# A third pair rearranged: its state products split over two visits, its values taken with the carried part, a quarter of w_out loaded plainly

## The chip, the cores and the metric

The kernel runs on one core of a Trainium2 chip. The metric is the time of one execution in microseconds (us) as the device measures it. TensorE (PE in the profile, PEld for its weight loads), VectorE (DVE), ScalarE (ACT), GpSimd (POOL) and SyncE (SP) each run their own list of instructions in order; SP and POOL also issue the DMAs.

## The reference

A block-wise linear attention with decay feeds a two-layer network. What is computed, shortened:

```python
# q, k, v: 4 batches, 8 heads, 768 tokens, 64 wide; blocks of 64 tokens
intra = (qb @ kb^T * Dmask) @ vb                 # Dmask[i, j] = lam ** (i - j) for i >= j, else 0
inter = (qb * lam ** (pos + 1)) @ kv_state
out_block = intra + inter
kv_state = lam ** 64 * kv_state + (kb * lam ** (63 - pos))^T @ vb
x = out, heads side by side                      # 3072 x 512
h = x @ w_in                                     # w_in: 512 x 2048
result = (h * cos(h)) @ w_out                    # w_out: 2048 x 512, result 3072 x 512
```

All inputs and the result are float32; the kernel multiplies in bfloat16.

## The kernel before, in words

**Tiling.** The 3072 tokens are 24 blocks of 128, taken two at a time: pair `pr` holds blocks `2*pr` and `2*pr+1`, the same chunk of two batches. Pairs 0 and 1 are made in another way ("spans", `add_span`). Pair 2 is the third pair, the first that goes the general way. The network works on tiles of `TILES = [4, 2, 2, 2, 2, 4, 4, 4]` blocks: tile 0 is the two spans, tile 1 is pair 2, tile 2 is pair 3, tile 3 is pair 4.

**One pair.** q, k and v of a block are loaded in float32 on SP's queue (L253, 256 KB each). q and v are scaled and all three become bfloat16 (`prepare`, L329 to L337; v as `v_s`). q and k are transposed into `qkT`, for pair 2 by TensorE (L359, 8 matmuls for q and 8 for k, copied out by DVE at L362), later by DMA (L365). On TensorE there follow: the scores (L407, 32 small matmuls), masked by DVE into `s_m` (L412); the state products, `update` (L419, 16 small matmuls for each 64-token half, "half 0" and "half 1"), added up by DVE (L425) into `sum` or into `S` in bfloat16; the values, half of them across the row halves of the output and half along them (`values` and the head of `values_carried`, L470, 16 small matmuls each); and the carried part, the state times q (L502). The output goes to `xT` (L510).

**One tile of the network.** `add_ffn`: `ps_h` = w_in times xT (L732, 16 groups of 4 matmuls), cos on ACT (L738), `g` on DVE (L744), then for each block `ps_f` = g times w_out (L779, 16 matmuls of 128x512, in groups of 4), copied to `o_sb` (L793) and stored. A group of 4 `ps_f` needs one quarter of w_out and four parts of g.

**Visits.** The pair's small matmuls use a quarter of the array, the network's all of it. A run of small matmuls between network matmuls is called a visit here. In the steady state one visit holds the values of a pair, the scores and state products of the next, and then the rest of the values and the carried part. Between the two halves of the values a 1x1 copy on DVE (`turn`, L487) must have read the first. Where a pair has no next one in its visit and no `turn`, `values_carried` puts a drain of TensorE there instead; no pair of the kernel before comes to that line.

**The third pair is special.** Its `add_stretch` is called with `ahead=first_update`: its first values share a visit with its own state products, and the second values share one with the carried part. Its scores follow the state product of the spans, L697. The state of the spans is copied by ACT (L701) and made bfloat16 by POOL (L704).

**Order of work.** A planner (`Planner.order`) sets each engine's order when the program is built: each step has a cost, what it depends on, a priority, PSUM banks and buffers, and the step that can start first is put next. `then` ties a step to the one that must follow it on its engine. The chip obeys only the order and the semaphores. `T_LAT` holds the planner's figures for the landing of the DMA transposes and thereby shifts where scores are placed.

**Loads.** `ORDER` names the early loads: q4, q5, k4, k5, v4, v5 are pair 2's blocks; i0 to i5 are w_in's parts and o0 to o3 w_out's quarters, issued by POOL, which turns float32 into bfloat16 during the DMA. o3 waits on POOL until q4 has landed, and SP issues v4 only when k4 has landed. q4 waits for a step of the network (`pace`).

Of the kernel before, what the change touches and what calls it, by code (L numbers as in the profile page):

```python
# [10 lines left out]
F32 = mybir.dt.float32  # L11
# [15 lines left out]
ALONE = [3, 4]  # L27
T_LAT = {3: 2.46, 4: 4.62, 5: 3.15, 6: 4.42, 7: 3.9, 8: 3.84, 9: 6.24, 10: 5.52, 11: 4.89}
HELD = (10,) * 12
# [7 lines left out]
STATE_OUT = [("ACT", "ACT"), ("ACT", "ACT")]  # L37
ORDER = "q0 k0 q1 k1 v0 v1 i0 i1 i2 i3 i4 i5 o0 o1 o2 q4 q5 k4 k5 o3"

# [107 lines left out]
def kernel(  # L147
# [127 lines left out]
    def add_load(n, name, src, prio, deps=()):  # L275
        b, c = where(n)

        def emit(_):
            t = loads.tile([P, H, D], F32, tag=name, name=name)
            live[name, n] = t  # L280
            i = start(nc.sync, t, src[b, :, c * P:(c + 1) * P, :].transpose([1, 0, 2]), deps)
            if (name, n) == ("q_f", 2 * SPANS):

                tc.add_manual_dep(i.ins, pace[0].ins.ins.name, mybir.DependencyInfo(
                    mybir.DependencyClass.Sync, mybir.DependencyReason.DATA), reason="order of loads")
            return i

        issue_t[name, n], load_t[name, n] = dma("SP", LOAD_US, 0.85, emit, prio, deps, get=name,
                                                lat=1.9 if name == "v_f" and n < 2 * SPANS + 2 else 1.0)
        return load_t[name, n]  # L290
# [3 lines left out]
    def add_w(which, c, prio, deps=()):  # L294
        def emit(_):
            if which == "in":
                a, z = sum(W_IN[:c]) * P, sum(W_IN[:c + 1]) * P
                return start(nc.gpsimd, w_in_sb[:, :, a:z], w_in_src[:, :, a:z], deps)
            a, z = c * KF // WCH, (c + 1) * KF // WCH
            return start(nc.gpsimd, w_out_sb[:, a:z, :], w_out_src[:, a:z, :], deps)  # L300

        part = W_IN[c] / 4 if which == "in" else 1.0
        early = which == "in" and c < 3
        _, w_t[which, c] = dma("POOL", 2.68 * part, 0.8, emit, -2000.0 if early else prio, deps,
                               lat=1.2)
        return w_t[which, c]

    T, So, Vo, d_t, Uo, Uo_sp = ({} for _ in range(6))
# [6 lines left out]
    def prepare(pr):  # L315
# [51 lines left out]
        for i, src in enumerate((a, k_)):  # L367
            get = None if i else "qkT"
            if 2 * pr >= DMA_FROM:
                head, T[pr, i] = dma("SP", 1.4, 1.3, partial(transposes_dma, i=i), 2 * pr + i - LAG + 1.5,  # L370
                                     src + ([qkT_head[pr]] if i else []), get=get, ordered=False)
                T[pr, i].lat = T_LAT.get(pr, 1.2)
                if i and 2 * pr + LAG < NBLK:
                    issue_t["q_f", 2 * pr + LAG].deps.append(head)
            else:
                t = pl.add("PE", MM(P, 8), src + ([T[pr, 0]] if i else []), partial(transposes, i=i), pa(-0.05 + 0.05 * i), banks=1)
                head = T[pr, i] = pl.add("DVE", 0.7, [t], partial(transposes_out, i=i), pa(0.0), get=get)
                t.bank_frees = [[head]]
            if i == 0:
                qkT_head[pr] = head  # L380
        qk_head[pr] = a[0]

    QUART = 0.0317
    first_sum = None

# [8 lines left out]
    def add_scores(pr, part):  # L394
# [3 lines left out]
        last, early = c == NB - 1, pr == SPANS  # L398
        nonlocal first_sum

        def scores(t):
# [11 lines left out]

        def update(t):
            live["kv", pr] = [bank(i, [P, H, D], F32, "ps_kv") for i in t.bank]
            for h in range(H):
                for s, r in enumerate(halves):
                    for m, kv in list(zip(halves, live["kv", pr]))[:1 if last else 2]:
                        nc.tensor.matmul(kv[r, h, :], lhsT=live["qk", pr][m, 1, h, s, :], rhs=live["v_s", 2 * pr + s][m, h, :],  # L419
                                         start=True, stop=True, skip_group_check=True)  # L420
# [15 lines left out]
        s_t.bank_frees = [[So[n0]], [So[n0 + 1]]]  # L436
        u = pl.add("PE", 8 * QUART, [s_t, d_t[n0], d_t[n0 + 1], v12.get(pr - 2)], update, part, banks=1 if last else 2)
        if early:
            u.deps.remove(s_t)
        else:  # L440
            s_t.then = u
        x = pl.add("DVE", 0.69, [u, Uo.get((pr - 1, 1)), Uo.get((pr - 1, 0))], partial(state, half=0, direct=last or early), pa(0.55))
# [3 lines left out]
        if early:  # L446
            x = first_sum = pl.add("DVE", 0.69, [x], partial(state, half=0), pa(0.56))
            u.bank_frees = [[x]]
        if not last:
            y = pl.add("DVE", 0.69, [x], partial(state, half=1), pa(0.57))  # L450
            u.bank_frees.append([y])
            for half, t in enumerate((x, y)):
                if (pr, half) not in Uo:
                    Uo[pr, half] = pl.add("ACT", 0.61, [t], partial(state_16, half=half), pa(0.56 + 0.02 * half))
        qk_head[pr].frees = [T[pr, 0], T[pr, 1], u]
        return s_t, u

    def add_stretch(pr, ahead=None):

# [29 lines left out]
        def values_carried(_):  # L489
            if not more and not apart and not ahead:  # L490
                nc.tensor.drain()
# [39 lines left out]
        apart = pr in APART  # L531
        if ahead:
            v1 = pl.add("PE", 4 * QUART + SW, [So[n0], So[n0 + 1]] + ahead.deps, values, ahead.prio, banks=2)
            v1.then = ahead
            ahead.deps.append(v1)
            chain = []
        else:
            v1 = pl.add("PE", 4 * QUART + SW, deps, values, pa(0.5), banks=2 + 2 * apart)
            chain = [v1]
        if more:  # L540
# [3 lines left out]
            chain += nxt  # L544
        if more or ahead:
            look = pl.add("DVE", 0.12, [v1], turn, pa(-9.0))
            look.worth = 0.45
            deps = deps + [look]
        v2 = v12[pr] = pl.add("PE", (12 if c else 8) * QUART + (SW if ahead else 0.0), deps, values_carried, pa(0.5))
        chain.append(v2)  # L550
# [9 lines left out]
        for s in range(2):  # L560
            So[n0 + s].frees = [v2]
            v_head[n0 + s].frees = [v2]
            if apart:
# [5 lines left out]
        qkT_head[pr].frees = [v2]  # L569
        if (pr + 1, 1) in Uo:  # L570
            Uo[pr + 1, 1].deps.append(v2)
# [144 lines left out]
    def add_ffn(i):  # L716
# [45 lines left out]
        for j in range(nb):  # L762
# [5 lines left out]
            for piece, part in enumerate(pieces):  # L768
                width = part.stop - part.start
                for f0 in range(0, KF, U4):  # L770
                    pr = begins[i + 1] + (j + f0 / KF) * nxt / nb + piece
                    if i == 0 and f0 == KF - U4:
                        pr = begins[i + 1] + (3.75 + 0.05 * j) * nxt / nb

                    def project(task, j=j, f0=f0, piece=piece, part=part, width=width):
                        if f0 == 0:
                            live["f", i, j, piece] = bank(task.bank[0], [P, DM], F32, "ps_f")
                        for f in range(f0, f0 + U4):
                            nc.tensor.matmul(live["f", i, j, piece][:, :width], lhsT=live["g", i][:, f, j * P:(j + 1) * P],  # L779
                                             rhs=w_out_sb[:, f, part], start=(f == 0), stop=(f == KF - 1))  # L780

                    t = pl.add("PE", MM(width, U4), [x for f in range(f0, f0 + U4) for x in gate[f]] + [w_t["out", f0 * WCH // KF], store],
                               project, pr, banks=0 if f0 else 1)
# [20 lines left out]

                eng, queue = ("DVE", "SP") if last and piece == 0 else ("ACT", "ACT" if last else "SP")
                e = pl.add(eng, 0.12 + width / 1060.0, [store], partial(project_out, eng=eng), begins[i + 1] + (j + 1) * nxt / nb,
# [11 lines left out]
    for at, name in enumerate(names):  # L818
# [3 lines left out]
        if name == f"q{2 * SPANS}":  # L822
            deps = []
        if name == f"v{2 * SPANS}":
            deps = [load_t["k_f", 2 * SPANS]]
        if name == "o3":
            deps = [load_t["q_f", 2 * SPANS]]
        if soft:
            kept.append(add_w({"i": "in", "o": "out"}[which], n, at, [] if at < 9 else deps))
# [8 lines left out]
    for pr in range(SPANS, NBLK // 2):  # L838
        prepare(pr)
    first_scores, first_update = add_scores(SPANS, prio_attn(2 * SPANS, 0.2))  # L840
    add_span_state(first_scores, prio_attn(2 * SPANS, 0.2))
    pr = SPANS
    for i in range(len(TILES)):
        while 2 * pr < first[i + 1]:
            if pr + 1 in ALONE:
                add_scores(pr + 1, prio_attn(2 * pr + 2, 0.2))
            add_stretch(pr, first_update if pr == SPANS else None)
            pr += 1
# [4 lines left out]
    closing.deps.append(v12[SPANS])  # L853
    first_sum.deps += Vo[2 * SPANS]
    lead_end = hid[2 * SPLIT]
# [81 lines left out]
```

## Time and profile before

| | |
|---|---|
| median of 3 runs | 202.2 us (201.93 to 202.43) |
| the profiled execution | 202.32 us, of which the span is 200.6 us |
| granted TensorE clock | 1.00 |
| DVE busy | 111.8 us (56%) |
| ACT busy | 116.3 us (58%) |
| POOL busy | 64.7 us (32%) |
| loads and stores of 256 KB on SP's queue | 79, among them 20 each of q, k, v |
| w_out's quarters on POOL's queue | 4, median 12.4 us to landing |

The span runs from the first to the last instruction in the record; 1.72 us lie around it. The ends of matmuls are modelled, their starts are recorded, so distances between starts are the safer reading. An engine's idle time costs something only if it reaches TensorE.

### The profile page before, as it was taken

What the parts mean: (1) busy time and instruction counts of PE and PEld (TensorE: products, weight loads), DVE (VectorE), ACT (ScalarE), POOL (GpSimd) and SP (SyncE); (2) the same over time, 40 slices, a digit from 0 to 9 for tenths busy, and PEclk for the clock granted to TensorE, in tenths of its full rate; (3) what the DMA queues carried; (4) which work ended last, traced back from release to release, by engine and by line L of the source; (5) the groups of instructions that cost most, each with busy time, mean ns of one, the idle gap of its engine ahead of it and who ended that gap; (6) DMA issues with size and microseconds to landing.
All of it is one profiled execution on the core that took longest, in us unless ns stands there. A gap on an engine that the chain in (4) does not pass through costs nothing.

```text
span 200.6 us, 5756 instructions
## 1 busy us (share of the span) xinstructions
PE 195.4 (97%) x2407; PEld 110.2 (55%) x2407; DVE 111.8 (56%) x211; ACT 116.3 (58%) x221; POOL 64.7 (32%) x85
## 2 busy tenths in 40 slices
PE   8799999999999999999999999999999999999994
PEld 2467444547758647867655454544445444444443
DVE  2978772258957816966735679367445454444001
ACT  5878771139768636948654878377455564345120
POOL 5793003066462636372736364003700000000000
DMA  5999999989997999999999899898921010111112
GB/s 161 305 191 204 203 199 215 174 197 227 218 213 172 198 222 199 216 204 187 220 192 242 154 226 178 232 394 197 260 83 51 6 52 3 52 52 52 52 56 105
DMA packets 96620, 33.93 MB, mean 169 GB/s; under 512 B 84690, under 2 KB 93650, under 8 KB 96594
## 3 DMA queue, kind: packets, MB, share of 16 engines
q1 hardware_dynamic: 89088, 28.78, 65.1%
q0 software_dynamic: 7360, 4.72, 16.5%
q8 instruction: 19, 0.31, 0.6%
q10 hardware_dynamic: 146, 0.07, 0.1%
q14 instruction: 7, 0.06, 0.1%
HBM read 27.26 MB, written 6.29 MB: 167 GB/s over the span
## 4 chain that ended last, share of the span: by engine, by line
PE 85%; DMA 9%; SPq 2%; DVE 1%; POOL 1%; ACT 0%; issue 0%; POOLq 0%
PE ps_h L732 41%; PE ps_f L779 36%; DMA v_f<-in_v_dram 4%; DMA sp_f<-in_k_dram 3%; SPq L253 2%; DMA k_f<-in_k_dram 2%; PE ps_o L470 2%; PE ps_o L502 2%; PE ps_kv L419 1%; PE ps_s L407 1%; PE ps_o L638 1%; PE ps_kv L625 1%; POOL k_sp L593 1%; DVE v_s L337 0%; PE ps_t L601 0%
## 5 line engine op out<-in xcount | busy, mean ns | idle before, releaser
L744 DVE TENSOR_TENSOR g<-ps_h,cos 128x256 bf16<-128x256 f32 (+1 forms) x133 | 70.4, 542 | 39.5 <-ACT cos L738 38.3
L779 PE MATMUL ps_f<-w_out_sb,g 128*128 128x512 bf16 (+2 forms) x400 | 90.5, 371 | 0.0
L732 PE MATMUL ps_h<-xT,w_in_sb 128*128 128x256 bf16 (+1 forms) x532 | 89.5, 320 | 0.0
L738 ACT ACTIVATE cos<-ps_h,halfpi 128x256 f32<-128x256 f32 (+1 forms) x133 | 72.1, 571 | 27.6 <-PE ps_h L732 26.3
L732 PEld LDWEIGHTS <-w_in_sb 128*128 128x128 bf16 x532 | 51.5, 98 | 32.9 <-DVE xT L510 0.4
L779 PEld LDWEIGHTS <-g 128*128 128x128 bf16 x400 | 37.5, 98 | 40.4
L329 POOL TENSOR_TENSOR qk<-q_f,q_scale 128x512 bf16<-128x512 f32 x19 | 19.5, 1045 | 38.1 <-DMA q_f<-in_q_dram 31.5
L793 ACT COPY o_sb<-ps_f 128x512 f32<-128x512 f32 (+1 forms) x24 | 13.8, 573 | 24.5 <-PE ps_f L779 24.4
L337 POOL TENSOR_TENSOR v_s<-v_f,v_scale 128x512 bf16<-128x512 f32 x19 | 19.7, 1044 | 10.5 <-DMA v_f<-in_v_dram 10.1
L510 ACT CAST xT<-ps_o 128x512 bf16<-128x512 f32 x15 | 8.1, 588 | 11.5 <-PE ps_o L502 9.1
L412 DVE TENSOR_TENSOR s_m<-ps_s,mask 128x512 bf16<-128x512 f32 x20 | 12.9, 684 | 3.3 <-PE ps_s L407 2.8
L333 POOL CAST qk<-k_f 128x512 bf16<-128x512 f32 x18 | 11.1, 614 | 6.2 <-DMA k_f<-in_k_dram 6.1
L425 DVE TENSOR_TENSOR sum<-sum,ps_kv 128x512 f32<-128x512 f32 x15 | 10.2, 680 | 0.6
L430 ACT CAST S<-sum 128x512 bf16<-128x512 f32 x15 | 9.1, 616 | 2.3 <-DVE sum L425 2.2
L487 DVE COPY spare<-ps_o 1x1 f32<-1x1 f32 x8 | 1.2, 156 | 15.3 <-PE ps_o L470 15.3
L253 POOL DMA_DIRECT2D w_out_sb<-in_moe_w_out_dram x4 | 3.0, 776 | 15.8 <-DMA q_f<-in_q_dram 15.8
L793 DVE COPY o_sb<-ps_f 128x384 f32<-128x384 f32 x1 | 0.6, 556 | 11.5 <-PE ps_f L779 11.5
L470 PEld LDWEIGHTS <-v_s 64*64 64x64 bf16 x320 | 4.2, 106 | 4.6 <-issue 3.2
L470 PE MATMUL ps_o<-s_m,v_s 64*64 64x64 bf16 x288 | 5.9, 197 | 0.1
L617 DVE TENSOR_TENSOR s_m_sp<-ps_s,mask_sp 128x512 bf16<-128x512 f32 x8 | 5.1, 682 | 1.3 <-PE ps_s L612 1.3
L864 PE MATMUL ps_idle<-const-float32-1.0 128*128 128x512 f32 (+1 forms) x6 | 4.8, 893 | 0.8 <-PEq L921 0.8
L502 PE MATMUL ps_o<-qkT,S 64*64 64x64 bf16 x304 | 5.1, 195 | 0.0
(75 smaller groups left out, 83.6 us busy)
## 6 DMA issues: line engine op xcount, KB each, us to landing
q_f<-in_q_dram SPq DMA_DIRECT2D x20, 256.0 KB, 3.8
k_f<-in_k_dram SPq DMA_DIRECT2D x20, 256.0 KB, 4.5
v_f<-in_v_dram SPq DMA_DIRECT2D x20, 256.0 KB, 4.8
out_dram<-o_sb SPq DMA_DIRECT2D x19, 256.0 KB, 2.8
w_out_sb<-in_moe_w_out_dram POOLq DMA_DIRECT2D x4, 512.0 KB, 12.4
sp_f<-in_q_dram SPq DMA_DIRECT2D x2, 512.0 KB, 5.0
sp_f<-in_k_dram SPq DMA_DIRECT2D x2, 512.0 KB, 5.5
w_in_sb<-in_moe_w_in_dram POOLq DMA_DIRECT2D x2, 512.0 KB, 8.8
```

The source lines that it names most:

```text
L329: vec[e].tensor_mul(new_qk()[:, 0, :, s], live.pop(("q_f", 2 * pr + s)), q_scale[:, c, :].unsqueeze(2).to_broadcast([P, H, D]))
L333: (nc.scalar.copy if early else nc.gpsimd.tensor_copy)(new_qk()[:, 1, :, s], live.pop(("k_f", 2 * pr + s)))
L337: vec[e].tensor_mul(live["v_s", 2 * pr + s], live.pop(("v_f", 2 * pr + s)), v_scale[:, c, :].unsqueeze(2).to_broadcast([P, H, D]))
L412: nc.vector.tensor_mul(t, live["s", pr][s], mask.unsqueeze(1).to_broadcast([P, H, D]))
L425: nc.vector.tensor_add(new, live["sum", pr, 0] if half else live["sum", pr - 1, 1], live["kv", pr][half])
L470: yield lambda h=h: nc.tensor.matmul(o[halves[h % 2], h // 2], lhsT=live["v_s", n0 + s][m, h, :], rhs=live["s_m", n0 + s][m, h, :], start= ...
L502: nc.tensor.matmul(live["o", n0 + s][halves[h % 2], h // 2, halves[half]], lhsT=S[r, h, :], rhs=live["qkT", pr][r, 0, h, halves[half]], st ...
L732: nc.tensor.matmul(t[:, :n], lhsT=w_in_sb[:, kd, f * P:(f + 1) * P], rhs=live["xT", i][:, kd, at], start=(kd == 0), stop=(kd == KD - 1))
L738: nc.scalar.activation(c[:, :n], live["h", i, f, at.start][:, :n], AF.Sin, bias=halfpi)
L744: return nc.vector.tensor_mul(live["g", i][:, f, at], live.pop(("h", i, f, at.start))[:, :n], live.pop(("c", i, f, at.start))[:, :n])
L779: nc.tensor.matmul(live["f", i, j, piece][:, :width], lhsT=live["g", i][:, f, j * P:(j + 1) * P], rhs=w_out_sb[:, f, part], start=(f == 0) ...
L793: (nc.scalar.copy if eng == "ACT" else nc.vector.tensor_copy)(o[:, :width], live["f", i, j, piece][:, :width])
```

## The change

- The third pair has no special values step any more. Its scores visit is now: the spans' state product, the scores, and the state product of **half 0** alone. The product of **half 1** moves into the scores visit of pair 3, behind pair 3's scores and ahead of pair 3's own state products.
- Its values and its carried part form one visit. There is no `turn` copy in it; the drain stands between the two halves of the values.
- w_out's last quarter is no longer one converting DMA of POOL. Four plain float32 loads on SP's queue (`w12` to `w15`, 256 KB each, rows of 2 KB) stand behind v5; ACT converts the first, POOL the other three. The last quarter's `ps_f` groups of tile 0 become two groups of two, (12, 13) and (14, 15), for each block.
- v4 is issued without waiting for k4.
- The k transposes of the third pair stand one group of 4 `ps_f` behind its q transposes, where it was two groups.
- One `o_sb` copy (tile 0, block 2) goes from ACT to DVE; the k transposes no longer wait for the copy of the q transposes; some figures of the planner change (`T_LAT`, latencies of loads).

In the built program TensorE's order between the first transposes and tile 1 is, in numbers of matmuls, before: L359 8, ps_f 8, L359 8, ps_f 8, L697 32, L407 32, ps_f 12, L470 16, L419 32, ps_f 4, L470 16, L502 32, ps_f 4. After: L359 8, ps_f 4, L359 8, ps_f 16, L697 32, L407 32, L419 16, ps_f 12, L470 32, L502 32, ps_f 4. Of the 12 `ps_f`, the first 6 use w_out parts 12 and 13, the last 6 parts 14 and 15. Later, pair 3's visit of L407 32, L419 32 becomes L407 32, L419 48, with one more group of 4 `ps_f` ahead of it; pair 4's scores stand 12 `ps_h` and 4 `ps_f` earlier. The numbers of matmuls are the same in all.

```diff
-ORDER = "q0 k0 q1 k1 v0 v1 i0 i1 i2 i3 i4 i5 o0 o1 o2 q4 q5 k4 k5 o3"
+ORDER = "q0 k0 q1 k1 v0 v1 i0 i1 i2 i3 i4 i5 o0 o1 o2 q4 q5 k4 k5 v4 v5 w12 w13 w14 w15"
+WF = ["ACT", "POOL", "POOL", "POOL"]
...
+    def add_w_plain(f, prio):
+        def emit(_):
+            live["w_f", f] = work.tile([P, DM], F32, tag="o_held", bufs=BUFS["o_held"], name="w_f")
+            return nc.sync.dma_start(out=live["w_f", f], in_=w_out_src[:, f, :])
+
+        issue, landed = dma("SP", 0.75, 0.6, emit, prio, get="o_held", lat=1.0)
+        e = WF[f - 12]
+        copy = nc.scalar.copy if e == "ACT" else nc.gpsimd.tensor_copy
+        cast = pl.add(e, 0.61, [landed], lambda _: copy(w_out_sb[:, f, :], live.pop(("w_f", f))), -1.0)
...
-                t = pl.add("PE", MM(P, 8), src + ([T[pr, 0]] if i else []), partial(transposes, i=i), ...)
+                t = pl.add("PE", MM(P, 8), src, partial(transposes, i=i), ...)
...
-        u = pl.add("PE", 8 * QUART, [s_t, d_t[n0], d_t[n0 + 1], v12.get(pr - 2)], update, part, banks=1 if last else 2)
+        sel = [0] if last or early else [0, 1]
+        u = pl.add("PE", 4 * QUART * len(sel), [...], partial(update, sel=sel), part, banks=len(sel))
+        s_t.then = u
         if early:
-            u.deps.remove(s_t)
-        else:
-            s_t.then = u
+            s_t.deps += [d_t[n0], d_t[n0 + 1]]
+        if second_update:
+            rest = second_update.pop()
+            s_t.then, rest.then = rest, u
...
         if not last:
-            y = pl.add("DVE", 0.69, [x], partial(state, half=1), pa(0.57))
+            u1 = pl.add("PE", 4 * QUART, [u], partial(update, sel=[1]), part, banks=1) if early else u
+            y = pl.add("DVE", 0.69, [x, u1], partial(state, half=1), pa(0.57))
+            if early:
+                second_update.append(u1)
...
         def values_carried(_):
-            if not more and not apart and not ahead:
+            if not more and not apart:
                 nc.tensor.drain()
...
-        if ahead:
-            v1 = pl.add("PE", 4 * QUART + SW, [So[n0], So[n0 + 1]] + ahead.deps, values, ahead.prio, banks=2)
-            v1.then = ahead
-            chain = []
-        else:
-            v1 = pl.add("PE", 4 * QUART + SW, deps, values, pa(0.5), banks=2 + 2 * apart)
-            chain = [v1]
+        v1 = pl.add("PE", 4 * QUART + SW, deps, values, pa(0.5), banks=2 + 2 * apart)
+        chain = [v1]
...
-                for f0 in range(0, KF, U4):
+                for f0, nf in [(0, 4), (4, 4), (8, 4), (12, 2), (14, 2)] if i == 0 else [...]:
...
-                eng, queue = ("DVE", "SP") if last and piece == 0 else ("ACT", "ACT" if last else "SP")
+                eng, queue = ("DVE", "SP") if last and piece == 0 or i == 0 and j == 2 else (...)
...
-        if name == f"v{2 * SPANS}":
-            deps = [load_t["k_f", 2 * SPANS]]
-        if name == "o3":
-            deps = [load_t["q_f", 2 * SPANS]]
```

## The prediction

> **What bounds the kernel now.** I read the page's busy times first, then the busy time in stretches, then TensorE's list of instructions where the change lies, then the chain of work that ended last, and last the DMA queues.
>
> ```profile
> PE 195.4 (97%) x2407; PEld 110.2 (55%) x2407; DVE 111.8 (56%) x211; ACT 116.3 (58%) x221; POOL 64.7 (32%) x85
> ```
>
> ```profile
> 30.00:35.00 5.00, 5.00 (x25) 2.26 (x24) 1.26 (x2) 0.62 (x1) 1.81 (x2) 1.00 1.04 216
> 35.00:40.00 5.00, 5.00 (x65) 2.91 (x63) 1.38 (x2) 0.62 (x1) 0.00 (x0) 1.00 1.05 171
> 40.00:45.00 5.00, 4.89 (x130) 2.43 (x126) 2.87 (x5) 1.86 (x4) 2.98 (x4) 1.00 0.87 198
> ```
>
> TensorE is busy in all of a span of 200.6 us but 5.2, and of the stretches from 20 to 180 us only 40 to 45 holds a hole, of 0.11. A busy TensorE is not always one at its best, so I checked the starts: a 128x512 `ps_f` takes 0.216 (24 in 5.18), from 29 us to the end. So little can be gained: the hole, and what a visit of small matmuls costs at its edges. Anything above that must be a new wait.
>
> TensorE around the change (start, us, operation, count):
>
> ```profile
> 34.99 0.61 PE L359 MATMUL ps_t<-ident,qk 128*128 128x128 bf16 x8
> 35.44 1.89 PE L779 MATMUL ps_f<-w_out_sb,g 128*128 128x512 bf16 x8
> 37.17 0.61 PE L359 MATMUL ps_t<-ident,qk 128*128 128x128 bf16 x8
> 37.62 1.89 PE L779 MATMUL ps_f<-w_out_sb,g 128*128 128x512 bf16 x8
> 39.44 0.69 PE L697 MATMUL ps_kv<-v_sp,k_sp 128*64 128x64 bf16 x32
> 40.06 0.44 PE L407 MATMUL ps_s<-qkT 64*64 64x64 bf16 x32
> 40.44 2.76 PE L779 MATMUL ps_f<-w_out_sb,g 128*128 128x512 bf16 x12
> 43.31 0.32 PE L470 MATMUL ps_o<-s_m,v_s 64*64 64x64 bf16 x16
> 43.46 0.43 PE L419 MATMUL ps_kv<-v_s,qk 64*64 64x64 bf16 x32
> 43.82 1.04 PE L779 MATMUL ps_f<-w_out_sb,g 128*128 128x512 bf16 x4
> 44.79 0.32 PE L470 MATMUL ps_o<-s_m,v_s 64*64 64x64 bf16 x16
> 44.94 0.46 PE L502 MATMUL ps_o<-qkT,S 64*64 64x64 bf16 x32
> 45.32 1.04 PE L779 MATMUL ps_f<-w_out_sb,g 128*128 128x512 bf16 x4
> ```
>
> The chain that ended last tells what made the hole: v5, late behind v4, whose issue waited for k4.
>
> ```profile
> 30.08 3.94 DMA k_f<-in_k_dram
> ...
> 34.51 7.98 DMA v_f<-in_v_dram
> 42.49 0.02 issue
> 42.51 0.75 DVE v_s L337
> ```
>
> **Part 1, the visit.** Two visits (43.31 and 44.79) become one. An entry costs 0.11: from 43.82 to 44.79 is 0.97 for four `ps_f` worth 0.86. An exit costs 0.10: L407 to `ps_f` is 0.38 (40.06 to 40.44), L407 to L419, inside a visit, 0.28 (53.31 to 53.59). One of each goes: -0.21. The state products only move: half 0 to the scores visit, half 1 to pair 3's, 16 matmuls of 8 ns each (32 in 0.26), together 0.
>
> **Part 2, the drain.** The joined visit has a drain after its first 16 values, and no row of before has one. The sixteen last 0.32 from first start to last end, and the next start now stands 0.15 behind the first; waiting for the end adds 0.17. The weight loads then start afresh (an L470 load takes 106 ns): +0.28. Bounds: 0, if the waiting hides in the matmuls' own pipeline (a wait can't gain), and 0.49, the whole 0.32 plus 0.11 for weights and 0.06 for a handover (v_s ended at 43.25, L470 began at 43.31). I take 0.28. Behind it on TensorE are 48 small matmuls and the closing `ps_f`; `xT` and tile 1 move with them.
>
> The Trainium skill, "TensorEngine Tiling (Array Packing)", Key Properties, says that a change of tiling mode drains TensorE. By that rule each edge of a visit should itself cost what a drain does, and the joined visit would gain 0.28 where I count 0.21. The edges here cost 0.10 to 0.11, so I stay with the rows.
>
> **Part 3, the hole.** `ps_f` x12 from 40.44, at 0.216 and an entry of 0.11, ends at 43.14; L470 started at 43.31: 0.17 waited for v5's `v_s`. With v5 early this goes: -0.17. What is late next decides the rest.
>
> **Part 4, the loads.** k5 was there at 35.46 (ACT, idle, began its cast at 35.48). v4 now follows at once; the spacing of such loads elsewhere is 1.27 (POOL's starts on q6, q7, k6, k7 and v6 run from 43.45 to 48.54, four steps). v4 is there at 36.7, v5 at 38.0; their casts end at 37.8 (POOL 1.04) and 38.8 (DVE 0.74). The scores visit, which now needs both, comes later (below): covered by 1.4.
>
> Then w12 to w15, 0.262 MB each in rows of 2 KB. No such load is in the trace. The nearest row is the span loads, 512-byte packets, alone on the engines from 5 to 8 us:
>
> ```profile
> DMA packets 2064, 1.04 MB, mean 347 GB/s; under 512 B 32, under 2 KB 2064, under 8 KB 2064
> ```
>
> That is 0.76 each; bounds: 0.67 at 394 GB/s (the best slice of the profile's 40, when stores run) and 1.27, the rate of 256-byte loads. I take 0.76, since rows of 2 KB are nearer to that row. w15 lands at 38.0 + 4 x 0.76 = 41.0 (40.7 to 43.1). POOL's cast of 0.61 (its L333 row) ends at 41.7.
>
> When does TensorE want it? From 34.99: q transposes to 35.44, one group to 36.30, k transposes to 36.75, 16 `ps_f` to 40.20, entry 0.1, L697 0.62, L407 0.28, L419 x16 0.13, exit 0.10: 41.4. Six `ps_f` with parts 12 and 13 end at 42.7, part 14 then, part 15 at 42.9. Allowing 0.06 for the handover, w15 may land as late as 42.2: 1.2 to spare at 0.76, 0.9 too late at 1.27.
>
> The skill's "DMA: Bandwidth & Descriptors", Rules for kernel authors, speaks against this part: a megabyte or more in one DMA, many small ones coalesced. Its fit in the anatomy section (2.0 us and the bytes at 436 GB/s, given for the software path) would make 2.6 us of each load, an estimate; one after another w15 would land at 48.4 and the kernel would lose over 5 us. The spacing of 1.27 between landings of 256 KB shows that such costs overlap on the queue, so I leave it out of the sum.
>
> POOL loses the issue of o3 (0.74) and gains three casts in time it idled (35.0 to 40.0 has nothing on POOL). Behind them stands the spans' S (0.61): 42.3, wanted at 44.1. ACT's one cast lies in its idle time before 40.17. SP issues four more loads, before q6: in sum the queue carries the same bytes, o3's now plain, and q6's old landing at 43.4 gives 2.4 after w15. Cost 0.
>
> **Part 5, k transposes earlier.** They are wanted at 36.30; k5's cast ended at 35.48 + 0.62 = 36.10. 0.2 to spare, and o3 no longer runs beside k5. Cost 0; if k5 is as late as a spacing of loads, 1.1.
>
> **Part 6, pair 3 and behind.** DVE must do mask, sum (half 1 of pair 2), mask and sum (pair 3) before ACT's S: in before's rows 0.65 and 0.70 to 0.75 each, 2.8, and 0.62 on ACT, 3.5 with handovers. Between pair 3's scores (0.3 after the visit's start) and its values lie 16 `ps_f` and the visit's rest, 4.0. Covered by 0.5. Pair 4's scores come 2.0 earlier, at 64.2; its DMA transposes were issued at 55.5 and 58.1 with up to 6.3 to land, 62.8 at the latest by their rows. Covered.
>
> **Sum.** -0.21 + 0.28 - 0.17 = -0.1. The profiled execution has 202.32 us (span 200.6 and 1.72 around it), so 202.2; the median of the runs shown is 0.12 below it, so **202.1 us**.
>
> **The rivals.**
> 1. *The drain is nearly free*: -0.38, 201.8. For it: visits are fed from work queued ahead. Against: nothing may start before the last value ends.
> 2. *The drain is dear*, 0.49: +0.1, 202.3. The change then doesn't do what it says: the edges saved come back as a drain.
> 3. *w_out's last quarter is late* (slower): each plain load takes 1.27. Part 15 is 0.9 late at the sixth of the 12 `ps_f` or next to it, and TensorE, which takes nothing out of order, stands: 202.1 + 0.9 = 203.0. It begins above 1.05 per load. For it: 1.27 is the only spacing that the trace shows on a long run of this queue. Against: 347 GB/s with rows a quarter as long.
> 4. *Another handover is late*: k5's cast (0.2 to spare) or DVE's chain in pair 3 (0.5). A delay of one small DVE or ACT step, 0.7: 202.8.
>
> **How the numbers follow.** Forecast 0.38, rival 1 0.17, rival 2 0.12, rival 3 0.20, rival 4 0.13. A measurement of this kernel tells some 0.3%, 0.6 us, from no change: below 201.6, above 202.8. Faster: 0.06 of rival 1 and 0.02 of the forecast, by the scatter of the runs, 0.08. Slower: 0.19 of rival 3, 0.08 of rival 4, 0.02 of rival 2, 0.29. The rest, 0.63, is the same. The range reaches from 201.5 (rival 1 and the runs' scatter of 0.3) to 203.2 (rival 3 with scatter); the forecast's own is 201.8 to 202.4.
>
> **What would show it.** The first `ps_h` of tile 1 at 46.1 instead of 46.22. No wait of TensorE's for DMA, POOL or ACT between 35 and 46. w12 to w15 landing 0.7 to 0.8 apart, the last at 41. One pause of 0.2 to 0.3 inside L470 x32. If the first `ps_h` stands right and the end does not, part 6 is wrong; if `ps_f` x12 takes over 3 us, rival 3 is right.

## The result and the profile after

The changed kernel takes 202.98 us (median of 6 runs, 202.79 to 203.11); beside it on the same chip the kernel before takes 202.29. The ratio is 1.0035 (95% interval 1.0022 to 1.0048): slower by 0.7 us, where 202.1 and no change was forecast. The profiled execution of the changed kernel has 202.79 us and a span of 201.0, 0.4 longer than before.

The busy times on the page, and then the busy time by stretches (the columns are stretch, its length, and busy time with the number of instructions of PE, PEld, DVE, ACT and POOL, then the granted clock, the DMA share and GB/s):

```profile
PE 193.4 (96%) x2382; PEld 110.7 (55%) x2407; DVE 112.0 (56%) x211; ACT 116.2 (58%) x221; POOL 65.4 (33%) x87
```

```profile
30.00:35.00 5.00, 5.00 (x26) 2.29 (x25) 1.16 (x2) 0.62 (x1) 1.04 (x1) 1.00 1.08 243
35.00:40.00 5.00, 4.95 (x36) 2.66 (x34) 2.08 (x3) 1.24 (x2) 1.65 (x2) 1.00 1.01 299
40.00:45.00 5.00, 4.85 (x157) 2.90 (x156) 3.17 (x5) 1.66 (x3) 4.02 (x6) 1.00 0.89 202
```

One trap first. TensorE seems two microseconds less busy than before, but 25 of its 2407 matmuls are missing from the record (x2382; the weight loads are still x2407). Where one is missing the trace shows "0.16 issue", as below at 45.30. It is no idle time: the distance between the starts around it is the same as elsewhere. I therefore read starts, and take the number of matmuls from the program's order.

TensorE around the change (start, us, operation, count):

```profile
34.90 0.61 PE L375 MATMUL ps_t<-ident,qk 128*128 128x128 bf16 x8
35.35 1.03 PE L801 MATMUL ps_f<-w_out_sb,g 128*128 128x512 bf16 x4
36.21 0.61 PE L375 MATMUL ps_t<-ident,qk 128*128 128x128 bf16 x8
36.66 3.62 PE L801 MATMUL ps_f<-w_out_sb,g 128*128 128x512 bf16 x15
40.20 0.69 PE L719 MATMUL ps_kv<-v_sp,k_sp 128*64 128x64 bf16 x32
40.83 0.45 PE L421 MATMUL ps_s<-qkT 64*64 64x64 bf16 x32
41.10 0.42 PE L434 MATMUL ps_kv<-v_s,qk 64*64 64x64 bf16 x16
41.46 2.76 PE L801 MATMUL ps_f<-w_out_sb,g 128*128 128x512 bf16 x11
44.15 0.74 PE L498 MATMUL ps_o<-s_m,v_s 64*64 64x64 bf16 x32
44.71 0.43 PE L530 MATMUL ps_o<-qkT,S 64*64 64x64 bf16 x32
45.30 0.81 PE L801 MATMUL ps_f<-w_out_sb,g 128*128 128x512 bf16 x3 [0.16 <-issue]
45.95 0.72 PE L754 MATMUL ps_h<-xT,w_in_sb 128*128 128x256 bf16 x5
```

There is no wait for a DMA, POOL or ACT, the joined visit stands at 44.15, and tile 1 begins at 45.95, 0.27 earlier than in the first trace of before. But 0.09 of that stands ahead of the change (the first transposes start at 34.90 and 34.99), and the rest is the hole of that one trace. The kernel before, run again without the hole, takes 11.05 us from its first transposes (35.00) to tile 1 (46.05); the changed kernel takes 11.05 too (34.90 to 45.95). So up to 46 us the change gains nothing. The place that does not look like the rest is one of 16 small matmuls: L434 x16 begins at 41.10 and the next `ps_f` at 41.46, as long as 32 of them take elsewhere. In pair 3's visit they cost more again:

```profile
53.90 0.45 PE L421 MATMUL ps_s<-qkT 64*64 64x64 bf16 x32
54.18 0.68 PE L434 MATMUL ps_kv<-v_s,qk 64*64 64x64 bf16 x48
55.01 3.40 PE L801 MATMUL ps_f<-w_out_sb,g 128*128 128x512 bf16 x15 [0.16 <-issue]
```

The net loss lies there, behind 46, and at the very end of the kernel.

To compare visits I use one measure, the **cost of a visit**: from its start to the start of the next one, less 0.2158 for each 128x512 matmul between them and 0.1092 for each 128x256 one, the mean distances of their starts in long runs. In us:

| | before | the kernel before, run again | after | the changed kernel, run again |
|---|---|---|---|---|
| spans' state, scores (with products of half 0 after) | 1.29 | 1.11 | 1.36 | 1.36 |
| values and carried part (two visits before) | 1.29 | 1.29 | 1.04 | 1.04 |
| pair 3's scores and products | 0.77 | 0.77 | 0.99 | 0.99 |
| last matmul's end to the end of the span | 2.86 | 2.88 | 3.11 | 3.11 |

### The profile page after: what moved, and what is told of

The parts are those of the page before. It is cut to its first block, busy times and chain, and to the rows that moved or that the text cites. A ratio compares the mean times of both kernels' runs of the same rounds, so it can differ in the third digit from the quotient of the medians.

```text
span 201.0 us, 5741 instructions
## 1 busy us (share of the span) xinstructions
PE 193.4 (96%) x2382; PEld 110.7 (55%) x2407; DVE 112.0 (56%) x211; ACT 116.2 (58%) x221; POOL 65.4 (33%) x87
## 3 DMA queue, kind: packets, MB, share of 16 engines
q1 hardware_dynamic: 89664, 29.83, 66.5%
## 4 chain that ended last, share of the span: by engine, by line
PE 92%; DMA 3%; issue 1%; SPq 1%; POOL 1%; ACT 0%; POOLq 0%
PE ps_h L754 41%; PE ps_f L801 41%; DMA sp_f<-in_k_dram 3%; PE ps_o L498 2%; PE ps_o L530 2%; PE ps_kv L434 2%; PE ps_s L421 1%; SPq L254 1%; PE ps_o L660 1%; PE ps_kv L647 1%; POOL k_sp L615 1%; PE ps_t L375 0%; PE ps_t L623 0%; PE ps_o L666 0%; PE ps_kv L719 0%
## 5 line engine op out<-in xcount | busy, mean ns | idle before, releaser
L801 PE MATMUL ps_f<-w_out_sb,g 128*128 128x512 bf16 (+2 forms) x381 | 86.8, 370 | 2.0 <-issue 1.4
L754 PE MATMUL ps_h<-xT,w_in_sb 128*128 128x256 bf16 (+1 forms) x526 | 88.4, 319 | 0.3
L815 ACT COPY o_sb<-ps_f 128x512 f32<-128x512 f32 (+1 forms) x23 | 13.1, 574 | 23.5 <-PE ps_f L801 23.4
L815 DVE COPY o_sb<-ps_f 128x512 f32<-128x512 f32 (+1 forms) x2 | 1.2, 624 | 11.9 <-PE ps_f L801 11.9
L498 PEld LDWEIGHTS <-v_s 64*64 64x64 bf16 x320 | 4.2, 106 | 4.4 <-issue 4.4
L498 PE MATMUL ps_o<-s_m,v_s 64*64 64x64 bf16 x288 | 5.9, 197 | 0.1
L434 PE MATMUL ps_kv<-v_s,qk 64*64 64x64 bf16 x288 | 4.9, 194 | 0.0
```

What stands on the lines that cost most here:

```text
L498: yield lambda h=h: nc.tensor.matmul(o[halves[h % 2], h // 2], lhsT=live["v_s", n0 + s][m, h, :], rhs=live["s_m", n0 + s][m, h, :], start= ...
L754: nc.tensor.matmul(t[:, :n], lhsT=w_in_sb[:, kd, f * P:(f + 1) * P], rhs=live["xT", i][:, kd, at], start=(kd == 0), stop=(kd == KD - 1))
L815: (nc.scalar.copy if eng == "ACT" else nc.vector.tensor_copy)(o[:, :width], live["f", i, j, piece][:, :width])
```

## The experiments

**Both kernels again, and two parts alone.** Three theories at this point: A, the loss is in the order behind 46 us; B, in the third pair's visits and the drain; C, in the plain loads. All four ran on one chip, where the kernel before had a median of 202.38.

> The changed kernel unaltered, for a second trace and a measure of the runs' scatter. Its first trace ends TensorE's work only 0.14 us later than before's, while the median is 0.69 us longer. If the loss is a marginal wait that strikes only some executions, this trace shows it (a pause of TensorE of 0.2 us or more that the first trace has not). If the loss is spread over many small steps, the landmarks of the two traces agree within 0.2 us. Median expected 202.8 to 203.1.

Measured: 202.89, ratio 1.0021 (1.0009 to 1.0034). The loss is 0.5 to 0.7, and the same places cost the same.

> The kernel before unaltered, for a second trace to set beside the first: 202.1 to 202.5 us, its landmarks on TensorE within 0.2 us of the first trace's. What differs between the two is scatter and no effect of the change.

Measured: 202.33, ratio 1.0009 (0.999 to 1.0028). The hole ahead of the first values (0.17 in the prediction, 0.18 by this measure) is not there: that visit costs 1.11, not 1.29.

The kernel before with nothing but the new `T_LAT`:

```diff
-T_LAT = {3: 2.46, 4: 4.62, 5: 3.15, 6: 4.42, ...}
+T_LAT = {3: 2.6, 4: 3.67, 5: 2.56, 6: 4.19, ...}
```

> The kernel before with only the planner's landing figures of the change: the first 46 us keep their order, but from tile 1 on pair 4's scores come earlier and groups of the network change places, almost as in the changed kernel. Theory A (the loss lies in the new order behind 46 us): 0.4 to 0.7 us slower than before. Theory B (it lies in the third pair's new visits and the drain) and theory C (it lies in the plain loads): within 0.2 us of before.

Measured: 203.03, ratio 1.0056 (1.0033 to 1.008). Its waits of TensorE hold one line that no other kernel of these four has:

```profile
PE ps_kv L419 <- DVE g L744: 0.7, 1, 0.7
```

The planner's new figures put scores and products of a later pair where DVE has not yet emptied a bank (in the visit at 119 us, cost 2.25 for 1.54). The changed kernel has no such wait: there the figures go with the other edits. So theory A's number came true here (0.65), by a wait that the changed kernel does not have.

The kernel before with the plain loads (w12 to w15 behind v5, v4 at once), its visits as they were:

```diff
-ORDER = "... q4 q5 k4 k5 o3"
+ORDER = "... q4 q5 k4 k5 v4 v5 w12 w13 w14 w15"
```

> The kernel before with w_out's last quarter as four plain loads behind v5 and v4 issued at once; the third pair's visits and the drain-free order stay as they were, but the planner moves some groups of the network. Theory C (the plain loads and the shifted queue cost the time): 0.4 to 0.7 us slower than before. Theories A and B: no slower, and up to 0.17 us faster, since the hole ahead of the first values closes.

Measured: 203.20, ratio 1.0048 (1.0034 to 1.0063). Two things in its trace. The planner, told of an earlier v5, places the values one step too early, and TensorE waits for the mask:

```profile
PE ps_o L486 <- DVE s_m L428: 0.5, 1, 0.5
```

And the end is 3.11 after the last matmul, as in the changed kernel. The second is common to the two kernels with the plain loads and to neither of the others. So the loss that theory A found is not the changed kernel's, C is right in a place where nobody looked, and what B says of the visits has to be priced. First the end: what does SP do there?

**The end of the kernel.** The last waits of SP's queue (engine, line, what it waited for: total, times, longest), first before, then after:

```profile
SPq L932 <- DMA out_dram<-o_sb: 1.4, 2, 1.0
SPq L932 <- PEq L932: 0.6, 2, 0.5
```

```profile
SPq L951 <- DMA out_dram<-o_sb: 1.6, 2, 1.3
SPq L951 <- PEq L951: 0.7, 2, 0.5
```

The sum differs by little; what stands behind it does. The trace records each wait of SP for semaphores there, two in one instruction (start in us, the semaphores; L932 and L951):

```
before                       after
197.85  115, 114             198.00  115, 114
197.92  100, 113             198.07  100, 113
197.99  103, 112             198.13  103, 112
198.05  104, 111             199.50  104, 111
198.12  106, 110             199.87  106, 110
198.17  107, 109             199.93  107, 109
198.24  116, 108             199.99  116, 108
199.32  117, 102             200.05  117, 102
199.72  118, 105             200.11  118, 105
```

SP goes through the list in a fixed order, 0.06 us for each. Transfers of SP and ACT take eight semaphores in turn (the first of each row from the second row on). Before, the last two stores have 117 and 118, the end of the list: all other waits are over by the time they land. After, four more transfers on SP's queue have moved the turn by four, the last stores have 104 and 106, and four waits of 0.06 are still to be made after the last landing. o3 was POOL's transfer and took none of the eight.

The test: four loads of 32 bytes more, late in the kernel, on SP.

```diff
+                    if n0 + j == 19:
+                        for z in range(4):
+                            nc.sync.dma_start(out=tiny[:, z, :], in_=lam.unsqueeze(0))
```

> The kernel before with four loads of 32 bytes more, issued by SP behind the store of block 19 (about 170 us), where SP has nothing else to do; no other engine has a different instruction or a different order. Theory T (the end): the semaphores that tell of finished transfers are taken in turn, eight of them, by SP's and ACT's transfers, and at the end SP waits for all of them in a fixed order. Four transfers more move the last two stores from the last two places of that order to the fourth and fifth, so four waits of 0.06 us each are still to be made when the last store has landed: from PE's end to the end of the span 3.11 in place of 2.87, the time up by 0.24 us (202.55 where the kernel before has 202.3), all else as before. Rival L (the loss of the changed kernel is behind 46 us, in visits and products; the end is longer there because its last store lands later): no difference, tail 2.87.

Measured: 204.25, ratio 1.0079 (1.0062 to 1.0096); the end 3.12 for 2.87.

> The changed kernel with the same four small loads at the same place, so that the last two stores take the last two semaphores again. Theory T: tail back from 3.11 to 2.87, the time down by 0.24 us, so about 202.7 where the kernel before has 202.3: slower by 0.4, not by 0.65. Rival L: no difference from the changed kernel (slower by 0.5 to 0.7), tail 3.11.

Measured: 204.85, ratio 1.0113 (1.009 to 1.0137); the end 2.85 for 3.11.

The end moved as theory T says, within 0.02. The times did not: both forms take 1.7 to 1.9 us more than the kernels they were made from, and their first w_out matmul stands at 30.0 and 29.8 instead of 28.9. `tiny` is a new tile of 128 bytes per partition ahead of the weights, so either the loads or the tile did it. Two runs without the tile (the loads go to unused columns of `spare`), and one with the room alone:

```diff
-    spare = consts.tile([P, 112], F32)
+    spare = consts.tile([P, 144], F32)
```

> The kernel before with the four small loads behind block 19's store again, now into unused columns of a tile that is there already, so that no tile in SBUF lies elsewhere (the first form added a tile of 128 bytes per partition ahead of the weights, and w_out's first matmul came 1.07 us later). Theory T: first w_out matmul at 28.9 to 29.0 as before, tail 3.11 in place of 2.87, the time up by 0.24 us to about 202.6. Rival L: no change, tail 2.87. Rival M (the small loads themselves make the start late, not the new tile): first w_out matmul at 30.0 again, the time up by 1.7.

Measured: 202.68 beside 202.36, ratio 1.0013 (0.9988 to 1.0037); first w_out matmul 29.17, the end 3.12. The waits of SP are those of the changed kernel:

```profile
SPq L935 <- DMA out_dram<-o_sb: 1.6, 2, 1.3
```

> The changed kernel with the same four loads into the same unused columns. Theory T: first w_out matmul at 28.9, tail 2.87, the time down by 0.24 us from the changed kernel: slower than the kernel before by 0.3 to 0.45, about 202.8. Rival L: slower by 0.5 to 0.7 as the changed kernel, tail 3.11. Rival M: slower by more than 2, first w_out matmul at 29.8.

Measured: 202.82 beside 202.36, ratio 1.002 (0.9998 to 1.0043); first w_out matmul 29.05, the end 2.86:

```profile
SPq L954 <- DMA out_dram<-o_sb: 1.4, 2, 1.0
```

> The kernel before with 128 bytes more per partition in a spare tile that lies ahead of the weights in SBUF; not one instruction is added. Theory P (where the tiles lie sets the rate of the first loads): 290 GB/s in place of 345 between 7 and 13 us, the first w_out matmul 1.0 us later, the time up by 1.0 to 1.7. Rival M (the four loads did it): 202.3, first w_out matmul at 28.95.

Measured: 204.0, ratio 1.0072 (1.0047 to 1.0096); first w_out matmul 29.92, the end 2.86.

So rival M falls: the room alone costs what both first forms lost. For T the medians alone would not do, since 0.24 us lies within their intervals; the traces do. In all sixteen of this study the end is 2.85 to 2.88 where SP and ACT issue the number of transfers of the kernel before, or eight more, and 3.11 to 3.13 where they issue four more, whichever kernel it is. The price of 0.25 is read from these traces.

**The products of one half.** The kernel before with the loops of `update` turned:

```diff
-            for h in range(H):
-                for s, r in enumerate(halves):
-                    for m, kv in list(zip(halves, live["kv", pr]))[:1 if last else 2]:
+            for m, kv in list(zip(halves, live["kv", pr]))[:1 if last else 2]:
+                for h in range(H):
+                    for s, r in enumerate(halves):
```

> The kernel before, with the loops of each state product turned: all sixteen products of one half of the tokens first, then all of the other half, where they alternated; same products, same banks, nothing else moved. Theory H (half rate): products that use one half of TensorE's rows alone start 15 to 16 ns apart, and 8 ns apart where the two halves alternate. Then each product of 32 takes 0.49 us in place of 0.25, 0.24 more in each of the nine or ten visits that hold one, 2.0 to 2.4 us in all: about 204.5. Rival E (the changed kernel's split product costs a second entry, or is late for another reason; the rate is the same): 202.3, and 32 products in 0.25 us as before.

Measured: 203.06, ratio 1.0038 (1.002 to 1.0055): slower by 0.6, between the two. Pair 3's visit, first in the kernel before run again, then here:

```profile
53.14 0.45 PE L407 MATMUL ps_s<-qkT 64*64 64x64 bf16 x32
53.41 0.46 PE L419 MATMUL ps_kv<-v_s,qk 64*64 64x64 bf16 x32
53.81 3.63 PE L779 MATMUL ps_f<-w_out_sb,g 128*128 128x512 bf16 x15
```

```profile
54.77 0.45 PE L407 MATMUL ps_s<-qkT 64*64 64x64 bf16 x32
55.04 0.58 PE L419 MATMUL ps_kv<-v_s,qk 64*64 64x64 bf16 x32
55.55 3.63 PE L779 MATMUL ps_f<-w_out_sb,g 128*128 128x512 bf16 x15
```

The products take 0.51 to the next start instead of 0.40. The single starts say why it is 0.11 and not 0.24. With alternating halves four matmuls start within 10 ns, then 22 ns pass: 31 ns for four. With one half there are two in 32 ns. But the second half's products do not wait for the last of the first half: from the eleventh start on the two halves run side by side. So the rate of theory H is right and its sum for this kernel was too large.

This profile also holds a wait of the old kind, and a large one, ahead of the third pair's first values:

```profile
PE ps_o L470 <- DVE v_s L337: 1.4, 1, 1.4
```

In the changed kernel nothing of the other half stands behind the sixteen products of half 0. To price them there, they were made twice:

```diff
-            for h in range(H):
+            for h in [h for h in range(H) for _ in range(2 if sel == [0] and pr == SPANS else 1)]:
```

> The changed kernel with the sixteen products of half 0 in the third pair's scores visit made twice, into the same places; nothing else is moved. Theory H (half rate): products of one half of the rows start 32 ns apart by pairs, so sixteen more cost 0.25, and the visit that begins at 40.2 goes from 1.36 to 1.61; the time is up by 0.25 on the changed kernel, about 203.1. Rival E (the rate is the same as for both halves, 8 ns, and the visit pays for something else, an entry or a wait): sixteen more cost 0.13, the visit 1.49.

Measured: 203.27 beside 202.40, ratio 1.0042 (1.0025 to 1.0058): slower than the kernel before by 0.87, where the changed kernel is slower by 0.5 to 0.7. The visit costs 1.61, as theory H says; rival E falls:

```profile
41.30 0.45 PE L421 MATMUL ps_s<-qkT 64*64 64x64 bf16 x32
41.57 0.68 PE L434 MATMUL ps_kv<-v_s,qk 64*64 64x64 bf16 x32
42.18 2.76 PE L801 MATMUL ps_f<-w_out_sb,g 128*128 128x512 bf16 x12
```

Thirty-two products of one half take 0.61 to the next start, sixteen take 0.36 (41.10 to 41.46 above): 0.25 for sixteen. Thirty-two of both halves take 0.40, less than sixteen of one and sixteen more. The Trainium skill, "TensorEngine Tiling (Array Packing)", Key Properties, says that tiles of the array work independently of each other, and Tiling Modes counts four of 64x64; two in 32 ns and four in 31 ns are what that looks like here.

**The product in one piece.** The changed kernel with both halves in the third pair's scores visit, and the four small loads in their first form:

```diff
-        sel = [0] if last or early else [0, 1]
+        sel = [0] if last else [0, 1]
```

> The changed kernel with the third pair's state product in one piece, both halves alternating, in its own scores' visit, and with the four small loads. The bank for the second half is free only one group of w_out later, so the planner puts the visit there and much of the later order comes out differently. Theories T and H: the fourth pair's visit costs 0.77 again in place of 0.99, the third pair's stays near 1.36 (1.11 with 16 more products at the full rate), tail 2.87: 0.45 less than the changed kernel, about 202.5, if the later order costs the same. Rival R (what the changed kernel loses is the order that the planner makes of the later visits): no nearer to the kernel before than the changed kernel, 203.0 or above, with waits in visits behind 100 us.

Measured: 205.36, ratio 1.0146 (1.0124 to 1.0167), of which the new tile brings some 1.6 (`b_pad`; the first w_out matmul is at 29.80). Pair 3's visit is back at 0.77 and the end at 2.86, as expected. The third pair's scores visit costs 1.85: the bank for half 1 is not free, and between its first product (42.40) and the next (42.88) TensorE stands (the second line here). A visit at 121 us has the wait of `b_tlat` again (the first line):

```profile
PE ps_kv L435 <- DVE g L763: 0.7, 1, 0.7
PE ps_kv L435 <- ACT sum L720: 0.3, 1, 0.3
```

So rival R has a part here, but not in the changed kernel. And without those waits it would hardly win either: if the scores visit then cost 1.36, as expected, 1.36 + 1.05 + 0.77 would be 3.18 for these visits, and the kernel before has 1.11 + 1.29 + 0.77 = 3.17.

**The drain by itself.** The kernel before, with a drain at the head of the third pair's `values_carried`:

```diff
-            if not more and not apart and not ahead:
+            if not more and not apart:
                 nc.tensor.drain()
```

> The kernel before with one explicit drain of TensorE ahead of the third pair's carried values, which stand behind the state products there; nothing else is moved. If the drain has the price that the prediction took, 0.28, the visit that holds the carried values costs 0.9 in place of 0.61 and the time goes to 202.6. Rival (the drain is nearly free where the engine has work queued behind it): 0.05, 202.3, and the pause of 0.29 in the changed kernel is then the handover between the two kinds of values.

Measured: 202.68 beside 202.36, ratio 1.0016 (0.9991 to 1.0042). The expectation described the place wrongly: one group of `ps_f` stands between the state products and the carried part there, so the drain waits for large matmuls. From `ps_f` to the next visit, first in the kernel before run again, then here:

```profile
43.87 0.81 PE L779 MATMUL ps_f<-w_out_sb,g 128*128 128x512 bf16 x3 [0.16 <-issue]
44.61 0.32 PE L470 MATMUL ps_o<-s_m,v_s 64*64 64x64 bf16 x16
```

```profile
44.75 0.81 PE L779 MATMUL ps_f<-w_out_sb,g 128*128 128x512 bf16 x3 [0.16 <-issue]
45.66 0.32 PE L470 MATMUL ps_o<-s_m,v_s 64*64 64x64 bf16 x16
```

0.74 becomes 0.91: the drain costs 0.17 at this place, neither 0.28 nor 0.05. This trace also reaches its first w_out matmul late, at 29.83, after a wait of 0.84 for `v_sp` long before the drain. In the changed kernel the drain stands among small matmuls, and the pause can be read directly: 0.292 from the start of the sixteenth L498 to that of the seventeenth, where the first sixteen start 8 ns apart on average. How much of it a handover between the two kinds of values would take without the drain was not tried.

**v4 early, alone.** The kernel before, in which v4 no longer waits for k4:

```diff
-            i = start(nc.sync, t, src[...].transpose([1, 0, 2]), deps)
+            i = start(nc.sync, t, src[...].transpose([1, 0, 2]), [] if (name, n) == ("v_f", 2 * SPANS) else deps)
```

> The kernel before with one thing of the change alone: v4 is issued without waiting for k4, so v5 is there earlier too; no other instruction and no order differs. Theory V (the hole ahead of the first values was mostly luck of that trace): no hole there, the visit that begins at 39.4 costs 1.11, and the median is at most 0.1 below the kernel before, 202.2 to 202.4, but runs above 203.5, which the wait for v5 makes, are gone. Rival G (the hole is there in most executions): 0.17 faster, 202.15. Rival C (an earlier v4 takes from k5's rate, as both then load together, and the k transposes wait): a wait of TensorE for k5's copy at 37, 0.3 to 0.7 slower.

Measured: 202.41 beside 202.40, ratio 1.0 (0.9991 to 1.0009). No hole, a cost of 1.11, and no gain in the median: theory V. The interval just reaches the 0.17 of rival G; what speaks against G is that six of eight traces with the old wait have no hole. Its 11 runs reach to 202.72; among 35 other runs of the kernel before two were above 203.7, but among the 17 beside this one none, so whether it spares the rare executions in which v5 is late is not shown. No version beat the kernel before.

## Why the prediction was wrong

Up to 46 us TensorE waits for nothing, as forecast. But the first `ps_h` at 45.95, near the forecast 46.1, is partly luck: what the joined visit saves, the scores visit spends, and the 0.27 come from an earlier start and from the hole of one execution. By the prediction's own terms tile 1 should have begun at 46.0, since half 1's 0.13 moves behind it. Its sum was wrong in three terms, and all three in one direction.

- **Part 1, edges: right.** The joined visit was to cost 0.61 + 0.67 - 0.26 (the products that leave) - 0.21 + 0.28 = 1.09; it costs 1.04.
- **Part 1, "the state products only move ... together 0": wrong, +0.21.** This is the step that failed on TensorE. The 8 ns of a product were read where both halves alternate. Split, sixteen of one half cost 0.25 and not 0.13: 1.36 - 1.11 = 0.25 in one visit, 0.99 - 0.77 = 0.22 in the other, 0.47 for 0.26 saved. `b_rows` shows the rate, `a_double` the price in place. The rate could have been seen before: pair 5's visit has sixteen products of one half alone, and in the trace of before they start 16.4 ns apart.
- **Part 2, the drain, +0.28: right**, by the pause of 0.292. At another place it costs 0.17.
- **Part 3, the hole, -0.17: wrong in size.** The term compared the change with one execution. Of eight traces with the old wait of v4, six have no hole (a cost of 1.11), the first has 0.18 and one (`b_rows`) a wait of 1.4. The change does take that wait away, but in a typical run there is nothing to take (`b_v4`: ratio 1.0, 0.9991 to 1.0009).
- **Part 4, the loads: right about landing, wrong about "Cost 0".** The last cast of w15 starts at 41.1 and takes 0.61, so it ends at 41.7 as worked out:

```profile
L314 SPq DMA_DIRECT2D w_f<-in_moe_w_out_dram x4: 429/431/1056, 34.0 to 36.1; - x4
L319 POOL CAST w_out_sb<-w_f x3: 612/614/615, 39.2 to 41.1; 128x512 bf16<-128x512 f32 x3
```

  The spacing was not 0.76 throughout: the casts that waited for a load begin at 38.41, 39.15 and 40.41, so one step is as long as the 1.27 of rival 3. Rival 3 is out all the same, since TensorE waits for none of them. But "SP issues four more loads" was counted as queue time alone. Their price is +0.25 at the end of the kernel, 160 us later, through the turn of the semaphores. No term of the sum and no rival had that place in it.
- **Parts 5 and 6: right.** No wait of TensorE for k5, DVE or `xT`; rival 4 is out. "If the first `ps_h` stands right and the end does not, part 6 is wrong" was too quick: part 6 held, and there were other places.

Together, against a run without the hole: 1.36 + 1.04 + 0.99 for 1.11 + 1.29 + 0.77 is +0.22, and +0.25 at the end makes +0.47. Measured were +0.69 and +0.51 (the two pairs of medians). What is left, 0.04 to 0.22, is open. In one pair of traces, both kernels run again (spans 201.17 and 200.52), it can be placed: +0.25 in the visits up to 74 us, +0.27 in those from 74 to 157, +0.23 at the end, and -0.10 by an earlier first w_out matmul. But the visits from 74 to 157 us scatter: they cost 9.89 to 10.04 in four traces of the new order (the changed kernel twice, `a_spare4`, `a_double`) and 9.70 in a fifth (`a_four`), and 9.70 to 10.01 in five of the old order (the kernel before twice, `b_spare4`, `b_v4`, `b_drain`). That is too much overlap to call it an effect of the new order, and not enough to exclude one of 0.1.

## What to carry to other kernels

A small matmul has no price of its own: it has one beside its neighbours. Before a group is split, look which parts of the array each piece uses, and take the duration from a row that uses the same parts. An edit that adds transfers has to be followed to the end of the kernel, where the waits for their semaphores are; count the transfers, not only their bytes. And a hole that one execution shows is a gain only if a second execution shows it too.

## What was not expected of the hardware

- The turn of the eight semaphores: four transfers more, of 32 bytes or of 256 KB, lengthen the end from 2.86 to 3.11, and eight more bring it back.
- 128 bytes per partition ahead of the weights, with no instruction added, cost 1.6 us (204.0 beside 202.36). The rate of the first loads, by fortieths of the stretch from 7 to 12 us, in the kernel before and then with the room:

```profile
GB/s 348 348 336 352 344 348 352 344 340 352 356 324 301 287 262 203 188 188 178 184 180 182 188 170 184 178 170 188 174 184 184 182 186 180 178 186 184 189 195 195
```

```profile
GB/s 287 291 279 307 279 295 291 262 319 274 311 279 299 287 283 299 274 307 274 285 260 219 180 188 182 182 186 176 190 180 182 180 172 170 182 182 186 178 188 180
```

  The loads run at some 290 GB/s for half of the stretch, where they ran at 345 for a third of it. From 7 to 9 us all four traces with the room show 290 or 291, the twelve others 324 to 333. In this trace 0.97 of the loss stands ahead of the first w_out matmul, and not all of that is the loads': TensorE too runs slower there, four transposes taking 0.61 and not 0.40, which `a_double` shows without the room (its first w_out matmul is at 29.33). `a_whole4` has the room and no slow transposes, and is still at 29.80. The rest of the 1.6 lies behind, and no run here places it. Why the place of the tiles matters was not tried. The Trainium skill, "DMA: Bandwidth & Descriptors", How a descriptor splits into AXI transactions, says that a read must start at a boundary of 256 bytes; it says this of what is read, and the tiles that moved here are written, so it does not explain the loss, and no run here varied the shift.
- Matmuls of 64x64 start 31 to 32 ns apart on one quarter of the array, and four quarters run at once; products of a second half overtake those of the first that still stand in line (the eleventh start on in `b_rows`).
